# Key scores of one batch computed beside the values of the batch ahead of it, and three small subtractions and products moved from GpSimd to VectorE

## The chip, the cores and the metric

The kernel runs on one core of a Trainium2 chip. The engines of the core that matter here are TensorE (in the profile PE for matmuls and PEld for the loading of their weights), VectorE (DVE), ScalarE (ACT), GpSimd (POOL) and SyncE (SP), which issues the DMAs. Each works through its own queue in the order in which the program was written, and waits for the others by semaphores. The metric is the device time in microseconds (us), the median of several runs.

## What is computed

Two stages, in float32. Agent attention: in each of 4 batches 49 agents take a weighted mean of 12480 values, and 12480 queries take a weighted mean of the agents' results. Then each of the 49920 tokens goes through a two-layer network with a squared ReLU of width 2048.

```python
B, N, C, n_agents = 4, 12480, 128, 49
def sm(a, b):
    s = scale * (a @ b.transpose(0, 2, 1))
    e = np.exp(s - s.max(-1, keepdims=True))
    return e / (e.sum(-1, keepdims=True) + 1e-09)
agent_v = sm(agents, k) @ v
x = (sm(q, agents) @ agent_v).reshape(B * N, C)
r = np.maximum(x @ w_in, 0.0)          # w_in: 128 x 2048
out = (r * r) @ w_out                  # w_out: 2048 x 128
```

## The kernel before

**The dense part.** Tokens are taken in 52 blocks of 960 (13 to a batch). The width of 2048 is cut into 16 slices, so that the main loop has 52 times 16 = 832 rounds. Round i does: `mm1` (line 467), 6 matmuls that give 128 hidden units of a block; `relu` and `square` on ScalarE (471, 475); `high` and `low` on VectorE (479, 483), which split the square g into a part gh that the fast float32 matmul takes exactly and the rest gl; and, six rounds later (`LAG`), `mm2` (495), 12 matmuls that add wo_hi·gh, wo_lo·gh and wo_hi·gl to the output of the block. `w_in` isn't used alone: for each batch `w_make` multiplies the agents' results into it, so that `mm1` takes the query weights (tiles p_a, p_b) directly. When a block's 16 rounds are over, `store_a` (506) and `store_d` (510) copy its two output banks out on ScalarE and VectorE.

**The attention part** is strewn between these rounds, in three strands:

- Keys of batch b, 13 pieces of 960: `k_pair` or `k_one` (scores on TensorE, line 195, into the only buffer of the tile ps_att), `kp_copy` (ScalarE, 212) into the score buffer sk, `kp_max` (VectorE, 217). When all pieces are there `k_max` makes the maximum.
- Values of batch b, the same 13 pieces: `k_sub` (GpSimd, 245) takes the maximum off, `k_exp` (ScalarE, 248), `k_hi` (VectorE, 252) and `k_lo` (GpSimd, 255) split the weight, `v_hi` (ScalarE, 262) and `v_lo` (VectorE, 266), each twice, split the value, `v_acc` (TensorE, 274) multiplies, `v_sum` (VectorE, 281) adds up.
- Queries of block s, two blocks ahead of their use: scores on TensorE (195), `q_max` and `q_sub` (VectorE, 386 and 392), `q_exp` (ScalarE, 401), `q_total` (VectorE, 405 to 409), `q_norm` (GpSimd, 412), `q_hi` (ScalarE, 420 and 421), `q_lo` (GpSimd, 425 and 426), `q_transpose` (TensorE, 436), `q_copy` (ScalarE, 442 and 443), `q_spread` (two small DMAs, 447 and 448).

sk holds the scores of one batch: 13 pieces, one buffer. So in each batch's 13 blocks the keys come first, some three blocks long, then the values, some nine blocks, then `w_make` for the next batch. Batch 0 is done ahead of the loop, and in blocks 0 to 38 the batches 1 to 3; the blocks from 39 on have queries alone.

**The order** is planned by the program itself. `at(t, f)` puts a step at the time t, counted in rounds, and all steps are written out in the order of t. `chain` finds slots for a string of dependent steps: it gives at most one step of a strand to each engine in each round (`taken`), adds a gap of rounds from engine to engine (`hop`), and keeps the rounds in which ps_att is held (`banks`). The rounds at the end of a block, where the output is copied, are kept free of it.

Two halves of a score tile are written by matmuls of different rows of the array; between them stands a no-operation on GpSimd (line 166), which waits for the first half and for which the second waits (`pass_on`, `take_over`); the same holds for the two halves of `mm2`.

Of the kernel before, what the change touches and what calls it, by code (L numbers as in the profile page):

```python
# [25 lines left out]
def agent_attention_relu2_kernel(ctx: ExitStack, tc: tile.TileContext, qT, kT, v, agT, w_in, w_out, outT):  # L26
# [509 lines left out]
    def chain(t, todo):  # L536

        first = prev = None  # L540
# [54 lines left out]
    def plan_batch(b, base, span):  # L595

        n = EARLY if b == 1 else 0
        while n < NS:
            m = min(2, NS - n)
            f = k_pair if m == 2 else k_one  # L600
            first, end = chain(base + int(n * KD), [("PE", f, b, n, 0), ("PE", f, b, n, 1), ("ACT", kp_copy, n, m), ("DVE", kp_max, n, m)])
            for x in range(m):
                at(max(base, first - 8 + x), k_load, b, n + x)
            n += m
        _, t0 = chain(end + 1, [("DVE", k_max, 0, NS), ("PE", k_max, 2), ("DVE", k_max, 3), ("PE", k_max, 4), ("DVE", k_max, 5)])
# [170 lines left out]
```

## Time and profile before

| | |
|---|---|
| median of 3 runs | 2016.65 us (2014.4 to 2017.15) |
| the profiled execution | 2010.7 us, its span 2008.7 us |
| time ahead of the first round's `relu` | 72.3 us |
| busy in the span: TensorE, VectorE, ScalarE, GpSimd | 1973.2, 1803.1, 1749.5, 334.7 us |
| granted TensorE clock, mean | 0.995 |

The profile was taken from one execution, so every time of a row belongs to the 2010.7 us; around its span of 2008.7 us lie 2 us. Lines are read as follows: a name such as "gl<-g,gh" says which tile an instruction writes and which it reads, "x832" how often it ran, and what stands in brackets or behind the last bar is how long the engine was idle before it and whom it waited for. In the view of windows each row is a stretch of time with the busy us of each engine in it.

### The profile page before, as it was taken

To read this page: it belongs to the slowest core of one execution; us is meant where nothing else is said; L and a number is where in the kernel's file an instruction comes from. 1 tells how busy PE (TensorE), PEld (TensorE's weight loads), DVE (VectorE), ACT (ScalarE), POOL (GpSimd) and SP (SyncE) were. 2 spreads that over 40 slices of the span, in tenths; PEclk is the share of its full clock that TensorE was granted. 3 is DMA by queue.
4 is the path that set the end of the run, shared out by engine and by line. 5 is a ranking of instruction groups with operands and counts; after the bars stand their busy time and mean duration, and the time that the engine had idled before them with its cause. 6 is when DMAs were issued, how large, how long until landed. Compare 5 with 4: busy or idle time off the path is not lost.

```text
span 2008.7 us, 47983 instructions
## 1 busy us (share of the span) xinstructions
PE 1973.2 (98%) x19835; PEld 1850.3 (92%) x19838; DVE 1803.1 (90%) x2306; ACT 1749.5 (87%) x2162; POOL 334.7 (17%) x261
## 2 busy tenths in 40 slices
PE   8999999999999999999999999999999999999998
PEld 7799999899989989999999999989998999999997
DVE  6787999999987899999988789999999889898987
ACT  2488999999987899999898789999998999999997
POOL 2110214123000012314100012322301010101000
PEclk9799999999999999999999999999999999999999
DMA  9421112120022112112012212112110010101000
GB/s 291 135 95 54 44 54 68 45 77 25 35 93 98 35 54 68 45 57 65 35 68 76 72 54 68 34 54 68 44 39 34 34 39 34 38 32 41 25 29 21
DMA packets 38502, 119.39 MB, mean 59 GB/s; under 512 B 4164, under 2 KB 11692, under 8 KB 38284
## 3 DMA queue, kind: packets, MB, share of 16 engines
q1 hardware_dynamic: 38284, 116.33, 18.4%
q8 instruction: 155, 2.54, 0.5%
q14 instruction: 63, 0.52, 0.1%
HBM read 80.97 MB, written 25.56 MB: 53 GB/s over the span
## 4 chain that ended last, share of the span: by engine, by line
PE 89%; DVE 6%; issue 3%; ACT 1%; POOL 0%; ACTq 0%; POOLq 0%; DVEq 0%
PE out L495 51%; PE h L467 26%; PE ps_att L195 7%; DVE gl L483 3%; PE ps_att L436 2%; PE ps_att L274 2%; DVE gh L479 1%; DVE vs L266 1%; PE ps_att L356 1%; DVE pe L252 0%; PE h L184 0%; DVE sk L245 0%; ACT ob L506 0%; ACT r L471 0%; PE out L632 0%
## 5 line engine op out<-in xcount | busy, mean ns | idle before, releaser
L483 DVE TENSOR_TENSOR gl<-g,gh 128x960 fp32r<-128x960 f32 x832 | 982.5, 1181 | 0.0
L471 ACT ACTIVATE r<-h 128x960 f32<-128x960 f32 x832 | 812.5, 977 | 167.0 <-PE h L467 138.3
L475 ACT ACTIVATE g<-r 128x960 f32<-128x960 f32 x832 | 835.5, 1004 | 18.4 <-DVE gl L483 16.9
L495 PE MATMUL out<-gh,wo_hi 64*128 64x480 f32 x3328 | 821.8, 388 | 10.6 <-ACT ob L506 9.3
L495 PE MATMUL out<-gl,wo_hi 64*128 64x480 f32 x3328 | 802.2, 377 | 9.5 <-DVE gl L483 9.4
L495 PE MATMUL out<-gh,wo_lo 64*128 64x480 f32 x3328 | 803.7, 377 | 0.0
L479 DVE CAST gh<-g 128x960 fp32r<-128x960 f32 x832 | 599.7, 721 | 152.1 <-ACT g L475 118.4
L495 PEld LDWEIGHTS out<-gh,wo_hi 64*128 64x128 f32 x3328 | 459.0, 184 | 44.2 <-ACT ob L506 16.5
L495 PEld LDWEIGHTS out<-gl,wo_hi 64*128 64x128 f32 x3328 | 460.0, 184 | 32.2 <-DVE gl L483 15.5
L495 PEld LDWEIGHTS out<-gh,wo_lo 64*128 64x128 f32 x3328 | 463.9, 186 | 13.0
L467 PE MATMUL h<-p_a,w_a 49*128 49x480 f32 x1664 | 409.8, 387 | 0.0
L467 PE MATMUL h<-p_b,w_a 49*128 49x480 f32 x1664 | 403.1, 377 | 0.3 <-DMA p_b<-p_a 0.3
L467 PE MATMUL h<-p_a,w_b 49*128 49x480 f32 x1664 | 403.3, 378 | 0.0
L467 PEld LDWEIGHTS h<-p_a,w_b 49*128 49x128 f32 x1664 | 231.7, 185 | 13.7
L467 PEld LDWEIGHTS h<-p_b,w_a 49*128 49x128 f32 x1664 | 233.6, 188 | 9.0 <-DMA p_b<-p_a 0.9
L467 PEld LDWEIGHTS h<-p_a,w_a 49*128 49x128 f32 x1664 | 230.0, 185 | 10.4 <-issue 1.5
L412 POOL TENSOR_TENSOR e<-e,sm 120x392 f32<-120x392 f32 x52 | 52.4, 1008 | 965.3 <-DVE gl L483 721.2
L425 POOL TENSOR_TENSOR pp<-e,pp 120x196 fp32r<-120x196 f32 x52 | 100.4, 1931 | 243.7 <-PE out L495 185.8
L195 PEld LDWEIGHTS ps_att<-ag_sb,qt 64*120 64x120 f32 x1632 | 113.9, 182 | 3.3 <-POOLq L166 1.0
L195 PE MATMUL ps_att<-ag_sb,qt 64*120 64x49 f32 x1632 | 106.9, 258 | 0.8 <-POOLq L166 0.8
L245 POOL TENSOR_TENSOR sk<-sk,mM 120x392 f32<-120x392 f32 x39 | 48.4, 1241 | 227.7 <-PE out L495 152.3
L195 PEld LDWEIGHTS ps_att<-ag_sb,kt 64*120 64x120 f32 x1248 | 79.4, 188 | 0.9
(133 smaller groups left out, 1169.6 us busy)
## 6 DMA issues: line engine op xcount, KB each, us to landing
kt<-kT SPq DMA_DIRECT2D x52, 480.0 KB
vt<-v SPq DMA_DIRECT2D x52, 480.0 KB
qt<-qT SPq DMA_DIRECT2D x52, 480.0 KB
outT<-ob SPq DMA_DIRECT2D x51, 480.0 KB
p_b<-p_a SPq DMA_DIRECT2D x104, 91.9 KB
raw<-w_in SPq DMA_DIRECT2D x4, 512.0 KB
raw<-w_out SPq DMA_DIRECT2D x4, 512.0 KB
outT<-ob SPq DMA_DIRECT2D x2, 240.0 KB
```

The source lines that it names most:

```text
L195: mm = nc.tensor.matmul(ps[:CH, u, r * A:(r + 1) * A], cols[u][r][rows], ag_sb[rows, b, :], start=x == 0 and r == 0, stop=x == 1 and r == ...
L245: eng.tensor_tensor(out=piece(n), in0=piece(n), in1=m.rearrange("p (o a) -> p o a", o=1).to_broadcast([CH, G, A]), op=ALU.subtract)
L274: nc.tensor.matmul(ps[:A2, t, :VW], pe[rows, c, :], vs[rows, c], start=c == 0, stop=c == G - 1)
L412: eng.tensor_tensor(out=es[s], in0=es[s], in1=sms.pop(s).to_broadcast([CH, G, A]), op=ALU.mult)
L425: eng.tensor_tensor(out=pp[:, :H, 64:], in0=e[:, :H], in1=pp[:, :H, :A].bitcast(F32), op=ALU.subtract)
L436: nc.tensor.matmul(ps[:M, t, c * n:(c + 1) * n], pps[s % 2][rows, c, :], ident_r[rows, rows], start=True, stop=True)
L467: nc.tensor.matmul(hs[i][:, t, :TT], w, p, start=n == 0, stop=n == 2)
L471: nc.scalar.activation(rs_[i], hs.pop(i)[:, :, :TT], AF.Relu)
L475: nc.scalar.activation(gs[i], rs_.pop(i), AF.Square)
L479: nc.vector.tensor_copy(ghs[i], gs[i])
L483: nc.vector.tensor_tensor(out=gls[i], in0=gs.pop(i), in1=ghs[i].bitcast(F32), op=ALU.subtract)
L495: mm = nc.tensor.matmul(o[u][:, :TT], w[rows, j, :], g[rows, u, :], start=j == 0 and x == 0 and n == 0, stop=j == NF - 1 and x == 1 and n ...
```

## The change

Three things are done.

1. The values of batch b and the keys of batch b+1 run side by side. `plan_batch` is split into `plan_keys`, `plan_maxima` and `plan_values`; behind every second piece of values, whose scores are then used up, stands a pair of pieces of the next batch's keys, which is copied into the same places of sk. The maximum of the next batch is made as soon as its last piece is there, and its values begin at once, where before they began after a stretch of keys alone.
2. `q_norm`, `q_lo` (in the loop) and `k_lo` run on VectorE. `q_hi` and `q_lo` take both halves of a block in one instruction each, by an access pattern (`swapped`) that reaches both. On GpSimd stay `k_sub`, a few steps around the start, and the no-operations.
3. In the planner: `SLACK`, the rounds left after GpSimd's steps, is gone; the last rounds of a block are kept from all strands but the steps named in `urgent`; in the start the second half of the queries' scores of block 1 stands half a round later, and the steps of `wo_make(2)` are moved.

```diff
     def q_hi(s):
-        pp, e = pps[s % 2], es[s]
-        nc.scalar.copy(pp[:, :H, :A], e[:, :H])
-        nc.scalar.copy(pp[:, H:, 64:], e[:, H:])
+        nc.scalar.copy(swapped(s % 2, 0), es[s].rearrange("p (t c) a -> p t c a", t=2))
 
     def q_lo(s, eng=nc.gpsimd):
-        pp, e = pps[s % 2], es.pop(s)
-        eng.tensor_tensor(out=pp[:, :H, 64:], in0=e[:, :H], in1=pp[:, :H, :A].bitcast(F32), op=ALU.subtract)
-        eng.tensor_tensor(out=pp[:, H:, :A], in0=e[:, H:], in1=pp[:, H:, 64:].bitcast(F32), op=ALU.subtract)
+        eng.tensor_tensor(out=swapped(s % 2, 64), in0=es.pop(s).rearrange("p (t c) a -> p t c a", t=2), in1=swapped(s % 2, 0).bitcast(F32), op=ALU.subtract)
...
-    taken |= {(e, s * NF + NF - 1 + LAG - x) for s in range(NSG) for e, n in (("ACT", 3), ("DVE", 2)) for x in range(n)}
+    kept = {(e, s * NF + NF - 1 + LAG - x) for s in range(NSG) for e, n in (("ACT", 3), ("DVE", 2)) for x in range(n)}
...
+    urgent = (kp_copy, kp_max, k_max, v_join, a_final)
...
-        _, ends[s] = chain(g + 1, [("ACT", q_exp, s), ("DVE", q_total, s), ("POOL", q_norm, s), ("ACT", q_hi, s), ("POOL", q_lo, s)])
+        _, ends[s] = chain(g + 1, [("ACT", q_exp, s), ("DVE", q_total, s), ("DVE", q_norm, s, nc.vector), ("ACT", q_hi, s), ("DVE", q_lo, s, nc.vector)])
...
-        _, end = chain(max(ends[s] + (1 if s < 3 else SLACK + 3), (s - 1) * NF), [("PE", q_transpose, s), ("ACT", q_copy, s)])
+        _, end = chain(max(ends[s] + 2, (s - 1) * NF), [("PE", q_transpose, s), ("ACT", q_copy, s)])
...
+    def plan_keys(b, n, t):
+        m = min(2, NS - n)
+        f = k_pair if m == 2 else k_one
+        first, end = chain(t, [("PE", f, b, n, 0), ("PE", f, b, n, 1), ("ACT", kp_copy, n, m), ("DVE", kp_max, n, m)])
+        for x in range(m):
+            at(max(0, first - 8 + x), k_load, b, n + x)
+        return end
...
+    def plan_values(b, t0, stop):
...
-            _, t1 = chain(max(t + (2 if n else 3), used.get(n - 3, 0)), [("ACT", k_exp, n), ("DVE", k_hi, n), ("POOL", k_lo, n)])
-            used[n], end = chain(max(t1 + SLACK, t2 + 2), [("PE", v_acc, n), ("DVE", v_sum, n)])
+            _, t1 = chain(max(t + (2 if n else 3), used.get(n - 3, 0)), [("ACT", k_exp, n), ("DVE", k_hi, n), ("DVE", k_lo, n, nc.vector)])
+            used[n], end = chain(max(t1, t2) + 2, [("PE", v_acc, n), ("DVE", v_sum, n)])
+            if b < B - 1 and n % 2:
+                plan_keys(b + 1, n - 1, t1 + 3)
...
-    at(.6, q_half, 1, 1)
-    at(.7, q_shift, 1)
+    at(1.02, q_half, 1, 1)
+    at(1.03, q_shift, 1)
...
     for b in range(1, B):
-        plan_batch(b, (b - 1) * NS * NF, NS * NF)
+        ready = plan_values(b, ready, b * NS * NF)
```

What this makes of the order is shown at three places. First VectorE's queue where the first two pieces of batch 1's values are split, before (L483 and L479 are `low` and `high`, L252 is `k_hi`):

```order
L252 CAST pe<-sk 120x8x49
L483 TENSOR_TENSOR gl<-g,gh 128x960
L479 CAST gh<-g 128x960
L252 CAST pe<-sk 120x8x49
L483 TENSOR_TENSOR gl<-g,gh 128x960
```

and now (L485 and L481 are the same `low` and `high`, L255 is `k_lo`):

```order
L252 CAST pe<-sk 120x8x49
L485 TENSOR_TENSOR gl<-g,gh 128x960
L481 CAST gh<-g 128x960
L255 TENSOR_TENSOR pe<-sk,pe 120x8x49
L485 TENSOR_TENSOR gl<-g,gh 128x960
L481 CAST gh<-g 128x960
L252 CAST pe<-sk 120x8x49
```

`k_lo` stands on VectorE now, a round behind its `k_hi`, with one `low` and one `high` between them. Second, GpSimd's queue at the same place, before (L412 is `q_norm`, L425 and L426 `q_lo`, L255 `k_lo`, L245 `k_sub`):

```order
L425 TENSOR_TENSOR pp_107<-e,pp_107 120x4x49
L426 TENSOR_TENSOR pp_107<-e,pp_107 120x4x49
L255 TENSOR_TENSOR pe<-sk,pe 120x8x49 x2
L245 TENSOR_TENSOR sk<-sk,mM 120x392
L412 TENSOR_TENSOR e<-e,sm 120x392
L255 TENSOR_TENSOR pe<-sk,pe 120x8x49
L245 TENSOR_TENSOR sk<-sk,mM 120x392
```

and now all that GpSimd computes from block 0's query weights on, to the end of the program (L303 and L121 belong to the start):

```order
L412 TENSOR_TENSOR e<-e,sm 120x392
L303 TENSOR_TENSOR ps_sum<-sk,ps_sum 120x8x49
L428 TENSOR_TENSOR pp_106<-e,pp_106 120x2x4x49
L121 TENSOR_TENSOR wo_lo<-wo_f,wo_hi 128x512 x4
L245 TENSOR_TENSOR sk<-sk,mM 120x392 x39
```

Of 234 instructions of the three strands on GpSimd in the loop only the 39 of `k_sub` are left, but for those of block 0. Third, TensorE's queue at the first two rounds, before (L467 is `mm1`, L195 the queries' scores):

```order
L467 MATMUL h<-p_a,w_a 128x480 x2
L467 MATMUL h<-p_b,w_a 128x480 x2
L467 MATMUL h<-p_a,w_b 128x480 x2
L195 MATMUL ps_att<-ag_sb,qt 120x49 x16
L467 MATMUL h<-p_a,w_a 128x480 x2
```

and now (L469 is `mm1`):

```order
L469 MATMUL h<-p_a,w_a 128x480 x2
L469 MATMUL h<-p_b,w_a 128x480 x2
L469 MATMUL h<-p_a,w_b 128x480 x2
L195 MATMUL ps_att<-ag_sb,qt 120x49 x8
L469 MATMUL h<-p_a,w_a 128x480 x2
L469 MATMUL h<-p_b,w_a 128x480 x2
L469 MATMUL h<-p_a,w_b 128x480 x2
L195 MATMUL ps_att<-ag_sb,qt 120x49 x8
```

The two halves of the queries' scores have the next round's `mm1` between them. In TensorE's order as a whole the 13 products of values (`v_acc`) of each batch stood in eight blocks before, 4 to 11, 17 to 24 and 30 to 37. Now those of batch 1 stand in blocks 4 to 11, those of batch 2 in blocks 14 to 24 and those of batch 3 in blocks 27 to 37. The keys of batch 2 stand in blocks 4 to 11 and those of batch 3 in blocks 15 to 24, where before they had blocks 13 to 15 and 26 to 28 to themselves.

More of the change, by code (lines that the diff above doesn't have):

```diff
@@ L416, in q_total, with swapped @@
         q_inverse(s)
+    def swapped(x, first):
+        pp = pps[x]
+        w = 64 + A
+        return bass.AP(pp.tensor, pp.offset + first, [pp.ap[0], [H * w + 64 - 2 * first, 2], [w, H], [1, A]])
     def q_hi(s):
[L419 to L421 removed]
+        nc.scalar.copy(swapped(s % 2, 0), es[s].rearrange("p (t c) a -> p t c a", t=2))
     def q_lo(s, eng=nc.gpsimd):
[L424 to L426 removed]
+        eng.tensor_tensor(out=swapped(s % 2, 64), in0=es.pop(s).rearrange("p (t c) a -> p t c a", t=2), in1=swapped(s % 2, 0).bitcast(F32), op=ALU.subtract)
     def q_transpose(s):
@@ L518, in agent_attention_relu2_kernel @@
     LAG = 6
-    SLACK = 5
-    KD, TAIL, EARLY = 3, 44, 4
+    TAIL, EARLY = 44, 4
     AHEAD = 3
@@ L542, in chain @@
             n = 1
-            while todo[0][0] == "PE" and n < len(todo) and (todo[n][1] in reads_bank and todo[n][0] != "PE" or todo[n][1:-1] == todo[n - 1][1:-1]):
+            while todo[0][0] == "PE" and n < len(todo) and (todo[n][1] in reads_bank and todo[n][0] != "PE" or todo[n][1:-1] == todo[n - 1][1:-1] and todo[n][1] is not k_max):
                 n += 1
@@ L547, in chain @@
                 g, p, ts = t, None, []
-                for e, *_ in todo[:n]:
+                for e, f, *_ in todo[:n]:
                     g += hop[p][e] if p else 0
-                    while (e, g) in taken:
+                    while (e, g) in taken or f not in urgent and (e, g) in kept:
                         g += 1
@@ L579, in plan_queries @@
         at(g + .5, q_shift, s)
-        _, ends[s] = chain(g + 1, [("ACT", q_exp, s), ("DVE", q_total, s), ("POOL", q_norm, s), ("ACT", q_hi, s), ("POOL", q_lo, s)])
+        _, ends[s] = chain(g + 1, [("ACT", q_exp, s), ("DVE", q_total, s), ("DVE", q_norm, s, nc.vector), ("ACT", q_hi, s), ("DVE", q_lo, s, nc.vector)])
     def plan_queries_early(s, base, loaded):
         first, ends[s] = chain(base, [("PE", q_half, s, 0), ("PE", q_half, s, 1), ("DVE", q_shift, s), ("ACT", q_exp, s), ("DVE", q_total, s),
-                                      ("POOL", q_norm, s), ("ACT", q_hi, s), ("POOL", q_lo, s)])
+                                      ("DVE", q_norm, s, nc.vector), ("ACT", q_hi, s), ("DVE", q_lo, s, nc.vector)])
         if not loaded:
@@ L590, in plan_turns, with plan_maxima @@
     def plan_turns(s):
-        _, end = chain(max(ends[s] + (1 if s < 3 else SLACK + 3), (s - 1) * NF), [("PE", q_transpose, s), ("ACT", q_copy, s)])
+        _, end = chain(max(ends[s] + 2, (s - 1) * NF), [("PE", q_transpose, s), ("ACT", q_copy, s)])
         at(end + .9, q_spread, s)
         assert end + 3 < s * NF, (s, end)
[L595 to L605, printed above, removed]
+    def plan_keys(b, n, t):
[5 more added lines that the diff above has]
+        return end
+    def plan_maxima(t):
+        _, end = chain(t, [("DVE", k_max, 0, NS), ("PE", k_max, 2), ("DVE", k_max, 3), ("PE", k_max, 4), ("DVE", k_max, 5)])
+        return end
+    def plan_values(b, t0, stop):
         used = {}
-        d = (base + span - TAIL - t0) / (NS - 1)
+        d = (stop - TAIL - t0) / (NS - 1)
         for n in range(NS):
@@ L707, in agent_attention_relu2_kernel @@
     at(.5, q_half, 1, 0)
-    at(.6, q_half, 1, 1)
-    at(.7, q_shift, 1)
-    _, ends[1] = chain(1, [("ACT", q_exp, 1), ("DVE", q_total, 1), ("POOL", q_norm, 1), ("ACT", q_hi, 1), ("POOL", q_lo, 1)])
+    at(1.02, q_half, 1, 1)
+    at(1.03, q_shift, 1)
+    _, ends[1] = chain(1, [("ACT", q_exp, 1), ("DVE", q_total, 1), ("DVE", q_norm, 1, nc.vector), ("ACT", q_hi, 1), ("DVE", q_lo, 1, nc.vector)])
     plan_turns(1)
@@ L731, in agent_attention_relu2_kernel @@
         plan_turns(s)
+    end = 0
+    for n in range(EARLY, NS, 2):
+        end = plan_keys(1, n, max(end - 1, 3 * n))
+    ready = plan_maxima(end + 1)
     for b in range(1, B):
-        plan_batch(b, (b - 1) * NS * NF, NS * NF)
+        ready = plan_values(b, ready, b * NS * NF)
     for i in range(NG + LAG):
```

11 lines of the change are left out of this document (7 added, 4 removed).

## The prediction

> **What bounds the kernel now.** I read the page's first part and its chain of waits first.
>
> ```profile
> PE 1973.2 (98%) x19835; PEld 1850.3 (92%) x19838; DVE 1803.1 (90%) x2306; ACT 1749.5 (87%) x2162; POOL 334.7 (17%) x261
> PE 89%; DVE 6%; issue 3%; ACT 1%; POOL 0%; ACTq 0%; POOLq 0%; DVEq 0%
> ```
>
> TensorE is the bound: 98% busy, 89% of the chain. The change takes no matmul away and adds none, so only time in which TensorE stands still can be won. The view of windows shows where it does. The first three rows are the nine blocks of values of batches 1, 2 and 3, the fourth is ten blocks with queries alone, the fifth one block with three pairs of keys.
>
> ```profile
> core 0: us, PE busy (x) PEld busy (x) DVE busy (x) ACT busy (x) POOL busy (x), PEclk, DMA share, GB/s
> 204.90:533.30 328.40, 322.51 (x3241) 305.36 (x3239) 315.80 (x403) 303.93 (x381) 86.33 (x53) 1.00 0.17 52
> 696.60:1025.40 328.80, 322.57 (x3241) 302.30 (x3239) 317.05 (x403) 303.93 (x382) 83.15 (x53) 1.00 0.17 51
> 1188.70:1517.70 329.00, 322.38 (x3240) 303.08 (x3238) 317.14 (x403) 304.17 (x381) 80.22 (x53) 1.00 0.17 52
> 1590.70:1930.60 339.90, 339.90 (x3365) 324.21 (x3362) 306.04 (x380) 318.26 (x380) 28.28 (x30) 1.00 0.10 35
> 613.00:657.20 44.20, 44.20 (x532) 43.07 (x530) 33.54 (x42) 34.36 (x42) 2.43 (x3) 1.00 0.24 79
> 905.47 1.14 PE L274 MATMUL ps_att<-vs,pe 56*98 56x258 f32 x16
> ```
>
> A block with queries alone costs TensorE 339.9/10 = 34.0 us, without a gap. A pair of keys adds (44.2 - 34.0)/3 = 3.4, also without a gap, and VectorE idles 10.7 of those 44.2 us. A piece of values adds 1.14 (last row, from the timeline). So the nine blocks of values should cost 9 x 34.0 + 13 x 1.14 = 320.8 us, and they cost 328.4, 328.8 and 329.0: 7.6, 8.0 and 8.2, together **23.8 us lost**. This is what can be won there. VectorE is busy 315.8 of 328.4 us in them, 96%. The timeline shows how a loss comes about:
>
> ```profile
> 237.29 1.42 DVE L479 CAST gh<-g 128x960 fp32r<-128x960 f32 x1
> 241.10 1.26 POOL L245 TENSOR_TENSOR sk<-sk,mM 120x392 f32<-120x392 f32 x1 [2.91 <-PE out L495]
> 241.47 1.91 DVE L483 TENSOR_TENSOR gl<-g,gh 128x960 fp32r<-128x960 f32 x1
> 243.43 0.19 PEld L495 LDWEIGHTS out<-gl,wo_hi 64*128 64x128 f32 x2 [1.19 <-DVE gl L483]
> 253.51 0.19 PEld L495 LDWEIGHTS out<-gh,wo_hi 64*128 64x128 f32 x2 [1.27 <-ACT ob L506]
> ```
>
> `high` takes 1.42 us and `low` 1.91 while GpSimd works; `mm2` then waits 1.19 for `low`, and some rounds later 1.27 for a late copy of the output. By line:
>
> ```profile
> L479 DVE CAST gh<-g x832: 641/660/1621, 78.9 to 1997.3; 128x960 fp32r<-128x960 f32 x167
> L483 DVE TENSOR_TENSOR gl<-g,gh x832: 1103/1148/1941, 84.0 to 1998.9; 128x960 fp32r<-128x960 f32 x167
> L479 DVE CAST gh<-g 128x960 fp32r<-128x960 f32 x832 | 599.7, 721 | 152.1 <-ACT g L475 118.4 <-PE h L467 27.6
> L483 DVE TENSOR_TENSOR gl<-g,gh 128x960 fp32r<-128x960 f32 x832 | 982.5, 1181 | 0.0
> L266 DVE TENSOR_TENSOR vs<-vt,vs x78: 674/680/1465, 225.5 to 1477.3; 120x512 fp32r<-120x512 f32 x78
> L266 DVE TENSOR_TENSOR vs<-vt,vs 120x512 fp32r<-120x512 f32 x78 | 59.6, 765 | 0.0
> L252 DVE CAST pe<-sk x39: 349/351/1123, 232.4 to 1469.2; 120x392 fp32r<-120x392 f32 x39
> L252 DVE CAST pe<-sk 120x392 fp32r<-120x392 f32 x39 | 16.1, 412 | 0.0
> ```
>
> The first row of each pair gives the shortest, median and longest, the second the mean (ns, ahead of the last bar). The medians are undisturbed, so the means show VectorE's loss: (721-660) x 832 + (1181-1148) x 832 + (765-680) x 78 + (412-351) x 39 = 51 + 27 + 7 + 2 = 87 us. GpSimd runs 52 + 104 + 39 + 39 = 234 of the strands' instructions, so each costs VectorE 0.37 us. The same loss stands in one longest `high`: 1.62 against 0.66.
>
> **The change, part by part.**
>
> *GpSimd to VectorE.* 51 `q_norm`, 51 `q_lo` (two became one) and 39 `k_lo`, 141 instructions of 392 elements, come to VectorE; 51 + 102 + 39 = 192 leave GpSimd. The trace has no such subtraction undisturbed at scale. From below bounds it the cast of 392 elements, 0.351; from above this:
>
> ```profile
> L245 DVE TENSOR_TENSOR sk<-sk,mM 120x392 f32<-120x392 f32 x7 | 5.4, 775 | 0.0
> L281 DVE TENSOR_TENSOR acc<-ps_att,acc 98x516 f32<-98x516 f32 x36 | 24.6, 683 | 0.0
> L217 DVE TENSOR_REDUCE pm<-ps_att 120x98 f32<-120x784 f32 x18 | 17.5, 975 | 9.1 <-ACT sk L212 9.1
> ```
>
> 0.775 is the same shape in the start, partly beside GpSimd. I take the line through two subtractions of the kind, (1.148 - 0.680)/(960 - 512) = 1.04 ns per element, so 0.680 - 120 x 1.04 ns = 0.555. VectorE gains 141 x 0.555 = 78 us of work and loses 192 x 0.37 = 71 us of disturbance: its total stays. In a block with queries alone 1.11 comes and 3 x 0.37 goes; TensorE still covers it, with 3.4 us of VectorE's idle time per block (306.04 of 339.90).
>
> The Trainium skill, "SBUF — State Buffer", section "SBUF: two separate sides", says that VectorE and GpSimd share a port pair as an exclusive lock: the loser blocks for the whole instruction. The rows above agree in kind. By that rule each of the 39 `k_sub` left could cost VectorE its whole length, 1.24 us, not 0.37; batch 3's margin below would then be gone, and the time about 2003.
>
> *Keys beside values.* A piece of values costs VectorE 2 x 0.680 + 0.351 + 0.683 (L281), now also 0.555, and 0.37 for its `k_sub`: 3.3 us. A pair of keys costs 0.975 (L217). Per block, over the base of 306.04/10 = 30.6:
> - batch 1, 9 blocks with 13 pieces and 7 pairs: VectorE 30.6 + 4.8 + 0.8 = 36.2; TensorE 34.0 + 1.65 + 2.45 (6.5 pairs of work) = 38.1.
> - batch 2, 11 blocks with the same: VectorE 30.6 + 3.9 + 0.6 = 35.1; TensorE 34.0 + 1.35 + 2.0 = 37.4.
> - batch 3, 11 blocks without keys: VectorE 34.5, TensorE 35.3.
>
> Before it was 315.8/9 = 35.1 against 320.8/9 = 35.6. The margin of 0.5 us per block, at which 0.85 a block was lost, becomes 1.9, 2.3 and 0.8; and single delays shrink, since bursts such as that at 237 to 243 came from several GpSimd instructions in a row, of which one is left. The loss lies between nothing and what it is. I take 1.5 us in batches 1 and 2 each and half of today's 8 in batch 3: **7 us left, 16.8 won**. The blocks of keys alone had no loss, so their end brings nothing by itself.
>
> *The start.* Here stands a wait:
>
> ```profile
> 73.82 1.27 POOL L121 TENSOR_TENSOR wo_lo<-wo_f,wo_hi 128x512 fp32r<-128x512 f32 x1 [22.86 <-ACT wo_hi L119]
> 73.85 1.73 PE L195 MATMUL ps_att<-ag_sb,qt 64*120 64x49 f32 x16 [0.84 <-POOLq L166]
> ```
>
> The second half of the scores waits 0.84 us for the no-operation, queued on GpSimd behind L121. With a round of `mm1` between the halves this is covered: 0.8 won. The two more VectorE steps here (1.1 us) replace about three disturbances (1.1).
>
> *The rest.* `q_hi` as one copy is ScalarE's gain, off the path: nothing. The queue of SP gets the same loads in another order; six buffers and 6 to 8 rounds of lead stay: nothing. The no-operations on GpSimd now wait behind one kind of work instead of four; their waits are within the loss above.
>
> *Sum.* 2010.7 - 16.8 - 0.8 = 1993.1 against the profiled execution. The median of the runs lies 6 us above it (2016.65); I put the same 6 on top: **1999 us**.
>
> **The rivals.**
>
> *The clock at the start.*
>
> ```profile
> 75.00:80.00 5.00, 5.00 (x41) 4.63 (x42) 4.14 (x8) 3.04 (x5) 0.27 (x2) 0.50 0.00 0
> 80.00:85.00 5.00, 5.00 (x46) 4.81 (x48) 4.92 (x7) 3.37 (x4) 2.00 (x2) 0.50 0.21 48
> 85.00:90.00 5.00, 4.39 (x17) 2.14 (x18) 3.40 (x5) 3.53 (x6) 0.00 (x0) 0.50 0.74 250
> ```
>
> After the wait of 0.84 the granted clock is 0.50 for these 15 us. If it stays up once the wait is covered, TensorE could win 7 us here; VectorE, busy 12.5 of the 15, lets through some 2.5 to 5: 1994 to 1997. For it: the wait precedes the drop. Against: scores, which follow, load the array little. The Trainium skill, "TensorE: Matmul & The Clock Gate", Part 1, has the clock halved after an idle window of some 3.4 us that runs freely; by that rule the drop can also fall elsewhere in any execution.
>
> *VectorE becomes the bound.* At 0.775 per added step VectorE's load per block grows by 0.22 x (2 + 13/11) = 0.7 in batch 3, whose margin falls to 0.1, and by about as much in the others. Then 8 us are lost in batch 3 and 2.5 in each of the others, 13 in all: 11 won, 2005; with heavier disturbance by `k_sub` besides, 2009. For it: VectorE's 96%. Against: the longest and shortest of that row (L245) were taken beside GpSimd's work.
>
> *Slower: ps_att.* It has one buffer, and the 14 pairs of keys now stand between products of values. If each pair held TensorE until `kp_copy` and `kp_max` behind a full VectorE queue are done, at 2 us a pair, 28 us come on and 17.6 go: 2027. It decides from 17.6/14 = 1.3 us a pair. For it, one such wait in the start:
>
> ```profile
> PEld ps_att L356 <- DVE pm L217: 1.3, 1, 1.3
> ```
>
> Against it: in 613.0 to 657.2 three pairs and the queries' uses ran without a gap, and the planner keeps ps_att a round longer than its last reader needs.
>
> *Nothing is won.* If the loss hangs on crowded rounds of ScalarE and VectorE, not on disturbance, the same crowding of values next to keys keeps it: 2013 to 2019.
>
> **How the numbers follow.** Forecast (1993 to 2005) 0.62; clock stays up 0.12; VectorE the bound 0.15 (two thirds of it still faster by over 0.2%); ps_att 0.05; nothing won 0.06. 0.2%, 4 us, is about what a measurement of this kernel can tell from no change. Faster 0.62 + 0.12 + 0.10 = 0.84, same 0.05 + 0.06 = 0.11, slower 0.05. The range runs from the clock's case, less the bound of a loss of nothing, to VectorE's case with `k_sub`: 1990 to 2010.
>
> **What would show it.** `high`'s mean near 0.67 and `low`'s near 1.155 us; GpSimd busy some 75 us; the added steps at 0.55; VectorE's total within 20 us of 1803; TensorE's waits for gl and ob nearly gone in blocks 3 to 38. It is wrong if waits for ps_att or for the no-operations appear, if the added steps take over 0.7, or if waits for gl persist without GpSimd beside them.

## The result, and the profile after

| | before | after |
|---|---|---|
| median of 6 runs each | 2015.32 us (2008.08 to 2017.15) | 1992.9 us (1987.12 to 2000.82) |
| ratio | | 0.9897, 95% interval 0.9866 to 0.9928 |
| profiled execution, its span | 2010.7, 2008.7 us | 1987.12, 1985.3 us |

The forecast was 1999 us, the range 1990 to 2010. The page of the changed kernel begins so (busy time, then the chain of waits):

```profile
PE 1967.1 (99%) x19838; PEld 1856.3 (94%) x19838; DVE 1791.3 (90%) x2447; ACT 1741.5 (88%) x2110; POOL 131.9 (7%) x68
PE 94%; DVE 4%; issue 1%; ACT 1%; DMA 0%; POOLq 0%; SPq 0%; DVEq 0%; ACTq 0%
```

TensorE's share of the chain rises from 89 to 94%, and VectorE's falls from 6 to 4. Where the time came from is read from the view of windows, cut at the `relu` of a block's first round: the rows are blocks 3 to 38. Columns as in the prediction's windows; of before

```profile
204.90:1555.51 1350.61, 1331.88 (x13595) 1252.75 (x13593) 1248.13 (x1582) 1214.92 (x1510) 273.36 (x186) 1.00 0.18 56
```

and of after:

```profile
201.57:1531.15 1329.58, 1325.86 (x13595) 1257.82 (x13593) 1233.83 (x1692) 1207.55 (x1474) 111.75 (x39) 1.00 0.18 57
```

The span is 23.4 us shorter. Blocks 3 to 38 give 1350.61 - 1329.58 = 21.0 of it, what lies ahead of them 204.90 - 201.57 = 3.3, and the end, from block 39 on, takes 1.0 back (454.19 for 453.23). In blocks 3 to 38 TensorE does the same matmuls (13595 records) and stands still for 1329.58 - 1325.86 = 3.7 us in place of 18.7; its busy time falls by 6.0 too. Why it does is not shown; in the runs below, too, it is higher where TensorE stands still for longer (1323.74 us with no standstill in e5b, 1340.57 with 26.1 in e12). VectorE's busy time stays near: 1248.13 and 1233.83.

TensorE's waits for the splits and the output copies, first of before, then of after (us in all, times, longest). The rows of PEld are waits of the weight loads, which can pass while matmuls still run; the rows of PE are those of the matmuls themselves. The last row of before is a wait of ScalarE's `square` for `low`:

```profile
PEld out L495 <- ACT ob L506: 16.5, 19, 1.4
PEld out L495 <- DVE gl L483: 15.5, 15, 1.5
PE out L495 <- DVE gl L483: 9.4, 12, 1.1
PE out L495 <- ACT ob L506: 9.3, 11, 1.0
PEld out L495 <- POOLq L166: 4.7, 9, 0.5
ACT g L475 <- DVE gl L483: 16.9, 24, 1.8
```

```profile
PEld out L497 <- POOLq L166: 9.1, 12, 2.1
PEld out L497 <- ACT ob L508: 3.6, 7, 0.9
PE out L497 <- POOLq L166: 3.2, 3, 1.7
```

Before, the two rows of PE make up nearly all of the 18.7 us: one half is `low` that came late, the other a late copy of the output on ScalarE, and ScalarE itself had stood 16.9 us for `low` (1.2 after the change). Now `mm2` has no wait for `low` left in the list, and for the output copy it waits 3.6 in place of 16.5. What has grown is the wait for the no-operation on GpSimd. The groups by line show why the waits for gl went, and what the moved steps cost (mean ns ahead of the last bar):

```profile
L485 DVE TENSOR_TENSOR gl<-g,gh 128x960 fp32r<-128x960 f32 x832 | 958.7, 1152 | 0.0
L481 DVE CAST gh<-g 128x960 fp32r<-128x960 f32 x832 | 559.0, 672 | 150.0 <-ACT g L477 86.9 <-PE h L469 58.5 <-PE ps_att L195 1.2
L412 DVE TENSOR_TENSOR e<-e,sm 120x392 f32<-120x392 f32 x51 | 28.5, 559 | 0.0
L428 DVE TENSOR_TENSOR pp<-e,pp 120x392 fp32r<-120x392 f32 x51 | 28.5, 559 | 0.0
L255 DVE TENSOR_TENSOR pe<-sk,pe 120x392 fp32r<-120x392 f32 x39 | 22.5, 578 | 0.0
L245 POOL TENSOR_TENSOR sk<-sk,mM 120x392 f32<-120x392 f32 x39 | 111.8, 2866 | 1200.9 <-PE out L497 689.2 <-DVE mM L242 374.0 <-ACT ob L508 54.3
```

`high` fell from 721 ns to 672 and `low` from 1181 to 1152. The one step left on GpSimd, `k_sub`, rose to 2866 ns from the 1241 of before:

```profile
L245 POOL TENSOR_TENSOR sk<-sk,mM 120x392 f32<-120x392 f32 x39 | 48.4, 1241 | 227.7 <-PE out L495 152.3 <-PE ps_att L195 51.3 <-DVE mM L242 24.0
```

### The profile page after: what moved, and what is told of

It reads as the page before. It is cut to its first block, busy times and chain, and to the rows that moved or that the text cites. A ratio compares the mean times of both kernels' runs of the same rounds, so it can differ in the third digit from the quotient of the medians.

```text
span 1985.3 us, 47656 instructions
## 1 busy us (share of the span) xinstructions
PE 1967.1 (99%) x19838; PEld 1856.3 (94%) x19838; DVE 1791.3 (90%) x2447; ACT 1741.5 (88%) x2110; POOL 131.9 (7%) x68
## 3 DMA queue, kind: packets, MB, share of 16 engines
q1 hardware_dynamic: 38284, 116.33, 18.7%
## 4 chain that ended last, share of the span: by engine, by line
PE 94%; DVE 4%; issue 1%; ACT 1%; DMA 0%; POOLq 0%; SPq 0%; DVEq 0%; ACTq 0%
PE out L497 54%; PE h L469 27%; PE ps_att L195 7%; PE ps_att L438 2%; PE ps_att L274 2%; DVE gl L485 1%; PE ps_att L356 1%; PE out L295 1%; DVE gh L481 1%; DVE sk L245 0%; PE h L184 0%; PE out L643 0%; DMA p_b<-p_a 0%; PE ps_one L184 0%; ACT r L473 0%
## 5 line engine op out<-in xcount | busy, mean ns | idle before, releaser
L485 DVE TENSOR_TENSOR gl<-g,gh 128x960 fp32r<-128x960 f32 x832 | 958.7, 1152 | 0.0
L497 PE MATMUL out<-gh,wo_hi 64*128 64x480 f32 x3328 | 920.8, 388 | 5.5 <-POOLq L166 3.2
L497 PE MATMUL out<-gh,wo_lo 64*128 64x480 f32 x3328 | 903.2, 377 | 0.0
L497 PE MATMUL out<-gl,wo_hi 64*128 64x480 f32 x3328 | 901.0, 376 | 0.0
L481 DVE CAST gh<-g 128x960 fp32r<-128x960 f32 x832 | 559.0, 672 | 150.0 <-ACT g L477 86.9
L497 PEld LDWEIGHTS out<-gh,wo_hi 64*128 64x128 f32 x3328 | 522.6, 184 | 32.7 <-issue 10.0
L497 PEld LDWEIGHTS out<-gh,wo_lo 64*128 64x128 f32 x3328 | 529.2, 186 | 11.0
L497 PEld LDWEIGHTS out<-gl,wo_hi 64*128 64x128 f32 x3328 | 525.7, 184 | 14.5
L469 PE MATMUL h<-p_a,w_a 49*128 49x480 f32 x1664 | 461.4, 386 | 0.0
L469 PE MATMUL h<-p_b,w_a 49*128 49x480 f32 x1664 | 454.9, 377 | 0.3 <-DMA p_b<-p_a 0.3
L469 PE MATMUL h<-p_a,w_b 49*128 49x480 f32 x1664 | 454.5, 378 | 0.0
L469 PEld LDWEIGHTS h<-p_a,w_b 49*128 49x128 f32 x1664 | 264.8, 185 | 19.6
L469 PEld LDWEIGHTS h<-p_b,w_a 49*128 49x128 f32 x1664 | 267.5, 188 | 8.0 <-DMA p_b<-p_a 0.9
L469 PEld LDWEIGHTS h<-p_a,w_a 49*128 49x128 f32 x1664 | 262.9, 184 | 9.5 <-issue 1.5
L245 POOL TENSOR_TENSOR sk<-sk,mM 120x392 f32<-120x392 f32 x39 | 111.8, 2866 | 1200.9 <-PE out L497 689.2
L195 PEld LDWEIGHTS ps_att<-ag_sb,qt 64*120 64x120 f32 x1632 | 119.3, 181 | 2.4 <-POOLq L166 0.5
L195 PE MATMUL ps_att<-ag_sb,qt 64*120 64x49 f32 x1632 | 113.0, 257 | 0.1
L195 PEld LDWEIGHTS ps_att<-ag_sb,kt 64*120 64x120 f32 x1248 | 80.8, 188 | 1.6 <-PE h L469 1.0
L195 PE MATMUL ps_att<-ag_sb,kt 64*120 64x49 f32 x1248 | 77.8, 267 | 0.6 <-PE h L469 0.6
L438 PEld LDWEIGHTS ps_att<-ident_r,pp 56*113 56x113 f32 (+1 forms) x816 | 57.2, 175 | 2.0 <-DVE pp L428 0.6
```

Of the source, the lines that this page charges most:

```text
L195: mm = nc.tensor.matmul(ps[:CH, u, r * A:(r + 1) * A], cols[u][r][rows], ag_sb[rows, b, :], start=x == 0 and r == 0, stop=x == 1 and r == ...
L245: eng.tensor_tensor(out=piece(n), in0=piece(n), in1=m.rearrange("p (o a) -> p o a", o=1).to_broadcast([CH, G, A]), op=ALU.subtract)
L438: nc.tensor.matmul(ps[:M, t, c * n:(c + 1) * n], pps[s % 2][rows, c, :], ident_r[rows, rows], start=True, stop=True)
L469: nc.tensor.matmul(hs[i][:, t, :TT], w, p, start=n == 0, stop=n == 2)
L481: nc.vector.tensor_copy(ghs[i], gs[i])
L485: nc.vector.tensor_tensor(out=gls[i], in0=gs.pop(i), in1=ghs[i].bitcast(F32), op=ALU.subtract)
```

## The experiments

Each kernel was compared with the kernel before on the same chip. "Blocks 3 to 38" means the window above, in that kernel's profiled execution.

| kernel | median us | ratio to before (95%) | blocks 3 to 38, us | TensorE still, us |
|---|---|---|---|---|
| before | 2015.32 | 1 | 1350.6 | 18.7 |
| after | 1992.9 | 0.9897 (0.9866 to 0.9928) | 1329.6 | 3.7 |
| e1, keys beside values alone | 1995.61 | 0.9887 (0.9849 to 0.9925) | 1334.9 | 5.0 |
| e2, engine moves alone | 1997.75 | 0.9903 (0.987 to 0.9936) | 1331.5 | 1.8 |
| e3, start alone | 2012.79 | 0.9995 (0.9978 to 1.0011) | 1354.2 | 19.0 |
| e4, after with idle work on GpSimd | 2038.26 | 1.0108 (1.0047 to 1.0169) | 1370.0 | 26.7 |
| e5, after with k_sub on VectorE, in part behind k_exp | 1991.29 | 0.9888 (0.9856 to 0.992) | 1326.3 | 1.2 |
| e5b, the same, k_sub ahead of k_exp | 1986.29 | 0.9881 (0.9849 to 0.9914) | 1323.7 | 0.0 |
| e6, e7, after with a warm start | 1999.55, 1991.93 | 0.9922, 0.9893 | 1329.6, 1329.6 | 3.7, 3.7 |
| e9, e2 with k_lo on GpSimd | 2010.02 | 0.9989 (0.9968 to 1.001) | 1347.9 | 13.6 |
| e10, e2 with q_norm, q_lo on GpSimd | 2023.86 | 1.0072 (1.0018 to 1.0127) | 1352.9 | 18.6 |
| e12, e2 with all three on GpSimd | 2038.97 | 1.0127 (1.0075 to 1.0179) | 1366.7 | 26.1 |
| e11, after with all three on GpSimd | 2038.56 | 1.0125 (1.0094 to 1.0156) | 1365.3 | 27.0 |

In these blocks the granted clock is 1.00 in every profile but two: e3's 1354.2 and e4's 1370.0 hold stretches at half clock, of which more below.

### One half of the change at a time

e1 is the changed kernel with the three steps planned and run on GpSimd again, with the rounds of slack behind them:

```diff
-("DVE", q_norm, s, nc.vector), ("ACT", q_hi, s), ("DVE", q_lo, s, nc.vector)
+("POOL", q_norm, s), ("ACT", q_hi, s), ("POOL", q_lo, s)
-("DVE", k_lo, n, nc.vector)
-max(t1, t2) + 2
+("POOL", k_lo, n)
+max(t1 + 5, t2 + 2)
-max(ends[s] + 2, (s - 1) * NF)
+max(ends[s] + (1 if s < 3 else 8), (s - 1) * NF)
```

> The new order of keys and values, but q_norm, q_lo and k_lo on GpSimd as before, with the five rounds of slack behind them. Blocks 3 to 38 (from the first relu of block 3 to that of block 39) take 1350.6 us before and 1329.6 after. Theory A, room: TensorE stopped because VectorE had only 0.5 us of room per block in the blocks of values, and the new order gives it more. Then most of the gain is here: 1330 to 1338 us, although VectorE's casts are disturbed as before (high's mean 0.72 us). Theory B, disturbance: TensorE stopped because several GpSimd instructions in a row stretched VectorE's, whatever the room. Then 1342 to 1349 us, with waits for gl and ob of 20 us or more in all.

e2 is the kernel before with the second and third part of the change but the start: the three steps on VectorE, `SLACK` gone, `kept` and `urgent`. Its keys still stand ahead of the values.

> q_norm, q_lo and k_lo on VectorE, without SLACK and with the rule on the last rounds of a block, but the keys ahead of the values as before. Theory A, room: VectorE's total stays and its room per block of values falls from 0.5 to 0.2 us, so nothing is won: blocks 3 to 38 at 1346 to 1358 us. Theory B, disturbance: high's mean falls to 0.67 us, the bursts are gone and most of the gain is here: 1330 to 1338 us.

e4 puts the disturbance back into the changed kernel by work on GpSimd that nobody reads, three sums of 392 elements per block and one per piece of values:

```diff
+    def idle_work():
+        nc.gpsimd.tensor_tensor(out=dum[0], in0=dum[0], in1=dum[1], op=ALU.add)
...
+            for x in range(3):
+                at(ends[s] - 2 + x, idle_work)
...
+            at(t1 + .6, idle_work)
```

> The changed kernel, and in addition on GpSimd three sums of 392 elements of a tile of its own for each block of queries and one for each piece of values, some 190 in all, which nothing waits for; nothing is taken off VectorE. high's mean should go from 0.672 towards 0.72 us and VectorE's busy time up by some 60 us, about 0.35 for each. Theory A, room: where room is over 1.5 us per block (batches 1 and 2) this costs little, in batch 3 (room 0.8) it costs some 4 to 8 us: blocks 3 to 38 at 1333 to 1340. Theory B, disturbance: stops come back in all three batches: 1343 to 1352.

The windows of blocks 3 to 38, below them the group of `high` and the wait of `mm2` for gl, of e1:

```profile
201.75:1536.67 1334.92, 1329.91 (x13595) 1254.11 (x13593) 1247.34 (x1582) 1211.28 (x1474) 214.69 (x150) 1.00 0.18 57
L481 DVE CAST gh<-g 128x960 fp32r<-128x960 f32 x832 | 615.7, 740 | 136.8 <-ACT g L477 103.4 <-PE h L469 27.8
PEld out L497 <- DVE gl L485: 1.9, 2, 1.5
```

Of e2, with its nine blocks of batch 1's values:

```profile
210.25:1541.78 1331.53, 1329.73 (x13593) 1246.66 (x13591) 1236.69 (x1693) 1210.49 (x1474) 92.40 (x39) 1.00 0.19 57
210.30:532.70 322.40, 321.85 (x3239) 298.45 (x3237) 312.59 (x435) 302.80 (x373) 30.78 (x13) 1.00 0.18 54
L481 DVE CAST gh<-g 128x960 fp32r<-128x960 f32 x832 | 563.4, 677 | 155.1 <-ACT g L477 94.7 <-PE h L469 57.1 <-PE out L497 1.0
```

Neither theory holds alone. e1 leaves `high` as disturbed as before (740 ns against 721) and still wins 15.7 us of the 21.0 in blocks 3 to 38. e2 leaves VectorE as full as before in the nine blocks of values (312.59 of 322.40 us, 97%), so it gives no room there at all, and wins 19.1. Together they win 21.0: each half does nearly all of it, and the gains do not add. The reading that fits both: before, a burst of held-up VectorE steps fell into blocks in which VectorE had no idle time to catch up, so `low` came late, and with it ScalarE's copy of the output. Without the burst there is nothing to catch up; with the keys spread out there is time to. That either half suffices is shown only together with what both runs hold: `q_hi` and `q_lo` as one instruction each and the rule of `kept` and `urgent`. No run has these two alone; against them speaks that e4 (below) has both, and its waits for gl and the output copy are back. That the backlog is the link is a reading of the waits: `mm2`'s for gl go in both (15.5 us before, 1.9 in e1, none listed in e2), and `square`'s for `low` shrink (16.9, 10.8, 4.5).

e4 ends beyond the kernel before, at 1370.0 us, and beyond both ranges expected. Its sums took 2131 ns each, and beside waits for gl (11.5 us) and for the output copy (18.9) it has waits for the no-operation of up to 5.5 us:

```profile
PEld out L497 <- ACT ob L508: 18.9, 29, 1.8
PEld out L497 <- POOLq L166: 16.6, 13, 5.5
PEld out L497 <- DVE gl L485: 11.5, 22, 1.3
```

So it cannot price the disturbance of VectorE by itself: work on GpSimd also delays the no-operations queued behind it. And some 7 us of the 1370.0, by an estimate, are the clock: in three stretches in which TensorE works for 14.8 us it is at half (below).

### The engine alone, in the same slots

In e2's program the three steps are written out exactly where they stand, but issued to GpSimd: `k_lo` (e9), `q_norm` and `q_lo` (e10), all three (e12); e11 does the same in the changed kernel.

```diff
-("DVE", k_lo, n, nc.vector)
+("DVE", k_lo, n)
-("DVE", q_norm, s, nc.vector), ("ACT", q_hi, s), ("DVE", q_lo, s, nc.vector)
+("DVE", q_norm, s), ("ACT", q_hi, s), ("DVE", q_lo, s)
```

> The kernel of e2 (keys ahead of the values, planner's new rules) with q_norm, q_lo and k_lo in exactly the slots of e2, but executed by GpSimd: the engine alone differs. Blocks 3 to 38 are 1331.5 us in e2 and 1350.6 in the kernel before. Theory B, disturbance: it is the engine, so the loss comes back: 1346 to 1356 us, high's mean 0.72 to 0.74. Theory E, planning: it is the new slots and the dropped SLACK, so it stays at 1331 to 1337.

> The kernel of e2 with k_lo alone executed by GpSimd, in the same slots (39 instructions). If the bursts of two k_lo beside k_sub do the harm, most of the 19 us between e2 and the kernel before comes back: 1340 to 1350 us for blocks 3 to 38. If each GpSimd instruction counts alike, 39 of 141 moved ones bring back some 5 us: 1335 to 1338.

> The kernel of e2 with q_norm and q_lo alone executed by GpSimd, in the same slots (102 instructions, of which 54 in the 27 blocks of values). The counterpart of e9: if the bursts of k_lo do the harm, 1332 to 1337 us for blocks 3 to 38; if each instruction counts alike, 1341 to 1346.

> The changed kernel with all three steps in its slots executed by GpSimd: the engine alone differs. Theory F, crowding: a stretched VectorE instruction stops TensorE only where several steps of values follow each other in neighbouring rounds, and the new order has fewer such places, so little comes back: blocks 3 to 38 at 1331 to 1338 us (1329.6 in the changed kernel, 1334.9 in e1 with SLACK). Theory B, disturbance: as much comes back as in e12, 1343 to 1352.

All four are slower than e2, three of them slower than the kernel before. Over e2, blocks 3 to 38 grow by 16.3 us (e9), 21.4 (e10) and 35.2 (e12); over the changed kernel by 35.8 (e11). e10 also loses 9.8 us in blocks 39 to 51 (464.0 against 454.2), where the kernel before, with the same steps on GpSimd, lost nothing. The wait of `mm2` for the no-operation, and one place in those blocks by the timeline (start, duration; in brackets the idle time and who ended it):

```profile
PEld out L497 <- POOLq L166: 53.0, 75, 1.4
```

```profile
1612.78 0.20 DVE L409 RECIPROCAL sm<-sm 120x8 f32<-120x8 f32 x1
1613.13 1.58 POOL L412 TENSOR_TENSOR e<-e,sm 120x392 f32<-120x392 f32 x1 [30.83 <-DVE sm L409]
1613.18 0.19 PEld L497 LDWEIGHTS out<-gh,wo_hi 64*128 64x128 f32 x2 [0.23 <-POOLq L166]
```

The no-operation that `mm2` needs in every round stands in GpSimd's queue behind `q_norm`, which itself waits for the reciprocal, and then behind `q_lo`, which waits for ScalarE. `mm2` goes on 0.05 us after `q_norm` starts, not when it ends: what it waited for was not GpSimd's work but GpSimd's turn. What GpSimd waited for ahead of `q_norm` differs accordingly, first in before, then in e10 (behind the last bar its idle time and what ended it):

```profile
L412 POOL TENSOR_TENSOR e<-e,sm 120x392 f32<-120x392 f32 x52 | 52.4, 1008 | 965.3 <-DVE gl L483 721.2 <-PE out L495 202.6 <-ACT r L471 40.9
```

```profile
L412 POOL TENSOR_TENSOR e<-e,sm 120x392 f32<-120x392 f32 x52 | 80.9, 1555 | 1174.5 <-DVE sm L409 989.0 <-PE out L497 93.2 <-PE ps_att L356 92.4
```

Before, the reciprocal had long been done when GpSimd came to the step, and such waits of TensorE came to 4.7 us; in e10 GpSimd came first and stood. In blocks 3 to 38 this wait of the matmuls is 17.8 of e10's 18.6 us of standstill, 22.8 of e12's 26.1 and 26.7 of e11's 27.0; in e9 it is 7.3 of 13.6, and 6.0 more are `v_acc`, which waits for `k_lo`. None of the four has a wait of `mm2` for gl in its list, though `high` is disturbed again (means of 688 ns in e9, 737 in e10, 752 in e11 and e12): it did not stop TensorE here, where TensorE already stood for GpSimd.

Three of the four lie outside both ranges that were expected; e9's 1347.9 lies in the one for bursts, but through these waits. The runs therefore do not separate the disturbance of VectorE from the wait for GpSimd, and the questions their expectations put (bursts of `k_lo` or each step alike) stay open. They show that the planning and the engine belong together: the tight slots are worth having only without GpSimd in the strand.

### What the changed kernel still loses

All of the 3.7 us but half a microsecond is one thing, three times. The three places in blocks 3 to 38 where TensorE waits for the no-operation, by the timeline of after (lines between them left out), are the starts of a batch's values:

```profile
1093.87 1.73 POOL L245 TENSOR_TENSOR sk<-sk,mM 120x392 f32<-120x392 f32 x1 [137.29 <-DVE mM L242]
1093.92 0.48 PE L497 MATMUL out<-gh,wo_hi 64*128 64x480 f32 x2 [1.68 <-POOLq L166]
613.02 0.49 PE L497 MATMUL out<-gh,wo_hi 64*128 64x480 f32 x2 [0.85 <-POOLq L166]
209.11 0.49 PE L497 MATMUL out<-gh,wo_hi 64*128 64x480 f32 x2 [0.69 <-POOLq L166]
```

The first `k_sub` of a batch waits at the head of GpSimd's queue for the maximum mM, with the no-operation of `mm2` behind it: 1.68 + 0.85 + 0.69 = 3.2 us. So `k_sub` was moved to VectorE as well. In e5 it stood in the slots planned for GpSimd, so that in some pieces the maximum is taken off behind the exponential: e5 thus computes something else, and its time tells of the load alone. e5b plans it ahead:

```diff
-            chain(max(t0, t - 4), [("POOL", k_sub, n)])
-            _, t1 = chain(max(t + (2 if n else 3), used.get(n - 3, 0)), [("ACT", k_exp, n), ...
+            _, ts = chain(max(t0, t - 6), [("DVE", k_sub, n, nc.vector)])
+            _, t1 = chain(max(t + (2 if n else 3), used.get(n - 3, 0), ts + 1), [("ACT", k_exp, n), ...
```

> The changed kernel with k_sub on VectorE too, so that GpSimd has nothing but the no-operations left in the loop. VectorE takes on 39 x 0.559 = 22 us and loses some 14 us of disturbance (high's mean 0.672 to 0.659). If load decides, batch 3 with the least room loses: blocks 3 to 38 at 1332 to 1336 us instead of 1329.6. If long single delays decide, it is 1327 to 1330 and the last waits for gl and ob go.

> The changed kernel with k_sub on VectorE too (39 more subtractions of 392 elements there, some 0.56 us each), planned six rounds ahead of k_exp, which follows a round behind it. GpSimd then has no work in blocks 3 to 38. Theory single delays (what was lost hung on delays by GpSimd's work, its no-operations among them): blocks 3 to 38 at 1326 to 1328 us (1329.6 with k_sub on GpSimd), no wait for a no-operation over 1 us in them, the mean of high at 0.66 and of low at 1.15, and the kernel within 0.3% of the changed one, ratio to before 0.986 to 0.991. Theory load (VectorE, 96 to 97% busy in the blocks of values, has no room for a further 0.56 us per piece): blocks 3 to 38 at 1333 to 1345, with waits of mm2 for gl.

The windows of e5b, blocks 3 to 38, and its group of `high`:

```profile
205.71:1529.45 1323.74, 1323.74 (x13595) 1260.87 (x13593) 1233.94 (x1731) 1207.84 (x1475) 0.00 (x0) 1.00 0.18 57
L481 DVE CAST gh<-g 128x960 fp32r<-128x960 f32 x832 | 546.8, 657 | 146.7 <-ACT g L477 84.4 <-PE h L469 55.6 <-PE ps_att L195 2.6
```

With GpSimd idle, TensorE doesn't stand still in 1323.74 us, and VectorE's busy time doesn't grow (1233.94 against 1233.83), as 39 steps of 0.56 us take the place of the disturbance. The theory of load falls, that of single delays holds, and stands even below its 1326. Against before, blocks 3 to 38 win 26.9 us, 5.8 more than the change. In timed runs e5b is the best of all, 0.9881, but its interval overlaps that of the change (0.9897), so that it is the faster of the two is likely and not shown.

### The start and the clock

e3 is the kernel before with the start's new order alone, `q_half` and `q_shift` half a round later and `wo_make(2)` behind them. e6 and e7 are the changed kernel with extra matmuls of `warm_up` strewn into the first six rounds, three or six to a round, whose products nobody reads.

> The kernel before, with only the start changed: the second half of the scores of block 1 behind the next round's mm1, and wo_make(2) moved. Theory C, cover: only the wait of 0.84 us goes, so the time is that of the kernel before within the spread of the runs (ratio 0.997 to 1.001), and what the profile of the changed kernel gained ahead of block 3 (204.9 to 201.6 us) was the luck of one execution. Theory D, clock: the covered wait keeps the clock up for a step or two of 3.4 us in most executions: ratio 0.995 to 0.998, 4 to 10 us less.

> The changed kernel with three dense bf16 matmuls of zeros in each of the first six rounds, 18 in all, which nothing waits for (some 4 us of TensorE at full clock). If the half clock of 13.7 us from 75 us on comes of too little dense work, it shrinks to a step or vanishes: blocks 0 to 2 at 124 to 128 us instead of 130.6, the runs closer together (within 5 us, not 14), and the median 3 to 8 us under that of the changed kernel. If not, blocks 0 to 2 at 132 to 136 us.

> As e6, with six such matmuls in each of the six rounds, 36 in all (some 8 us at full clock). If the clock stays up with three already, these add up to 4 us to e6; if three are too few and six enough, blocks 0 to 2 at 126 to 130 us and the median under that of e6.

e3 wins nothing that can be measured (0.9978 to 1.0011). The stretch from 70 to 100 us, of before, e3, after and e7 in turn (the third number from the end is the mean granted clock):

```profile
70.00:100.00 30.00, 28.14 (x248) 23.23 (x249) 22.35 (x33) 18.73 (x25) 4.91 (x5) 0.72 0.18 55
```

```profile
70.00:100.00 30.00, 23.54 (x266) 18.63 (x266) 23.54 (x35) 20.48 (x27) 4.85 (x5) 0.89 0.22 67
```

```profile
70.00:100.00 30.00, 28.17 (x268) 22.30 (x267) 22.59 (x36) 20.15 (x26) 2.54 (x2) 0.77 0.18 56
```

```profile
70.00:100.00 30.00, 28.39 (x239) 16.81 (x241) 21.19 (x39) 17.50 (x23) 2.55 (x2) 1.00 0.25 77
```

In e3's profiled execution the clock is higher here than before, and block 3 begins 2.6 us earlier (202.3), but over 12 runs nothing of it is left. Its blocks 3 to 38 are 3.6 us longer, and this is the clock as well: from 470.8 to 477.6 us it is at 0.50, right behind a standstill of TensorE.

```profile
470.39 0.95 PE L495 MATMUL out<-gh,wo_hi 64*128 64x480 f32 x2 [1.57 <-ACT ob L506]
470.80:477.60 6.80, 6.80 (x45) 5.93 (x46) 5.29 (x7) 2.46 (x4) 0.00 (x0) 0.50 0.19 75
```

In e4 the same happens three times: at 250.8, 384.0 and 640.0 us the clock falls to 0.50 for 6.9, 6.8 and 3.4 us, within a standstill of 5.15 us, at the end of one of 1.43 and 0.3 us behind one of 1.64. But 1.68 us in after and 2.53 in e4 left it at 1.00. A standstill of TensorE can thus cost more than its own length; which ones do is not shown.

In e7 the clock stays at 1.00 from 74 us on. From the first `relu` to block 3 after takes 130.6 us, e6 131.7 and e7 132.6: what the full clock gives there, the extra matmuls take. Neither of the ranges expected with a gain (124 to 128 and 126 to 130) came true. e7 ends where the change does (0.9893), e6 a little behind, within the noise. What a full clock at the start would be worth without extra work stays open.

## Why the prediction was right, and where it was off

**The bound and the place: right.** Only time in which TensorE stands still could be won, and it was won in blocks 3 to 38: 21.0 of 23.4 us.

**What could be won, 23.8 us: a little small.** e5b, without any standstill in blocks 3 to 38, puts it at 1350.6 - 1323.7 = 26.9.

**The price of a moved step, 0.555 us: right.** 559, 559 and 578 ns. The rival of 0.775 falls with it. Its total on VectorE: 1791.3 for 1803.1 us, within the 20 named.

**The disturbance, 0.37 us per GpSimd step: right for this kernel, in part by luck.** The same sum over after's means gives (672 - 660) x 832 + (1152 - 1148) x 832 + (693 - 680) x 78 + (356 - 351) x 39 ns = 14.5 us, over 39 `k_sub` 0.37 each; 356 is the mean of `k_hi`, and the 693 is from this row of after:

```profile
L266 DVE TENSOR_TENSOR vs<-vt,vs 120x512 fp32r<-120x512 f32 x78 | 54.1, 693 | 0.0
```

But the price is no constant. By the same sum a GpSimd step costs VectorE about 0.4 us in e2, 0.5 in e1 and e9, and 0.65 in e10, e11 and e12 (with 39, 180 and 78, and 141, 180 and 180 such steps). Nor is the longest `high`, 1.62 against 0.66 before, "The same loss": that is 0.96 in one step.

The Trainium skill, "SBUF — State Buffer", section "SBUF: two separate sides", makes the loser of the shared port wait for the winner's whole instruction. On average VectorE lost far less than the 1.24 us per `k_sub` that the prediction worked out by it, and in the longest `high` (1.42) and `low` (1.92) of after some 0.77; the one that was held up for longer was GpSimd (below).

**The loss left, 7 us: the term that was mis-sized.** The prediction took 1.5 us each for batches 1 and 2 and 4 for batch 3, whose margin of "room" it put at only 0.8 us a block. Three stretches of nine blocks, read from after, one in each batch's values:

```profile
201.60:543.90 342.30, 341.47 (x3654) 326.37 (x3652) 317.29 (x438) 307.52 (x380) 24.81 (x13) 1.00 0.22 68
693.60:1028.70 335.10, 335.10 (x3546) 325.06 (x3545) 310.03 (x427) 302.34 (x371) 36.51 (x10) 1.00 0.20 62
1175.20:1493.40 318.20, 317.84 (x3196) 303.41 (x3196) 303.92 (x420) 298.45 (x364) 26.16 (x10) 1.00 0.16 49
```

TensorE stands still for 0.8, 0.0 and 0.4 us; the waits of 0.85 and 1.68 us for the maximum lie ahead of the second and the third stretch. In batch 3 VectorE is 303.92/318.20 = 96% busy, as before the change, and nearly nothing is lost. So small a margin cost next to nothing here once the bursts were gone, which e2 (97%) and e5b say too. So 21.0 us were won there in place of 16.8; the mechanism named beside it ("single delays shrink") was the one to price.

**The start, 0.8 us: covered as said, worth nothing measurable** (e3). The 3.3 us of the two profiles are not shown to be a gain of the change: e3 and after begin block 3 at 202.3 and 201.6 us, e5 and e5b at 204.2 and 205.7 with the same start.

**The sum.** Against the profile the working gave 1993.1; it was 1987.12, 6.0 less: 4.2 from the loss left and 2.5 from the start, less the 1.0 that the end took, and 0.3 around the span and in rounding. The 6 us put on top for the median came true (it lies 5.8 above the profiled execution), but in part by luck: the profiled execution is the fastest of the six, and the median stands between two groups of three (1987 to 1990 and 1996 to 2001).

**What was not foreseen.** By the prediction's own words it is wrong if waits for the no-operations appear. They did, in small: those of the matmuls of `mm2` went from none listed to 3.2 us. GpSimd's busy time was to fall to some 75 us and is 131.9; most of the difference is `k_sub`, at 2866 ns where its old 1241 would have made 63 us less. The no-operations' waits, "within the loss above" by the prediction, are nearly all that is left of the loss.

**The rivals.** That ps_att holds TensorE falls: the waits of TensorE for `kp_max` are 2.0 us in all against 1.3, and none of them lies in blocks 3 to 38. That crowding keeps the loss falls with e2. That the clock would bring a gain with the start's order does not show in e3's runs. VectorE as the bound falls with the 0.56 us of the moved steps and with e5b.

## What to carry to other kernels

A nearly full engine cost nothing here as long as its steps came at their usual length. Price the bursts that lengthen them, and the idle time that absorbs a burst: taking away the bursts, or adding the idle time, each won most of the loss here, and both together little more. If an engine's queue also carries no-operations that order other engines, each step on it that waits for its input holds those up: plan such a step so that its input is ready, or take it off that queue.
